# Attention and a squared-ReLU feed-forward layer on one core: the scores of a tile written as two operations, and a new order of all work

## The chip, the cores and the metric

The kernel runs on one core of a Trainium2 chip. The metric is the time of one execution on the device in microseconds (us). Each version is run several times, and the median of its runs is its time.

## The reference

Two things are computed, one after the other. First, attention with 4 batches, 8 heads, 768 tokens and 64 numbers per head. A token sees the first 8 tokens of its batch ("global" keys) and itself with the 95 tokens before it ("local" keys):

```python
scores = (1.0 / np.sqrt(D)) * np.matmul(q, k.transpose(0, 1, 3, 2))
rel = pos[:, None] - pos[None, :]
is_global = pos[None, :] < 8
is_local = (rel >= 0) & (rel < 96)
keep = is_global | is_local
dist = np.where(is_global & ~is_local, 96.0, np.abs(rel))
scores = scores - slopes[:, None, None] * dist        # slopes[h] = 2 ** -(h + 1)
a = softmax(np.where(keep, scores, -1e9))
attn = np.matmul(a, v)                                # (4, 8, 768, 64)
```

Then the result, with the heads side by side, is a matrix x of 3072 tokens by 512, and goes through a feed-forward layer:

```python
h = x @ w_in                  # (3072, 512) @ (512, 2048)
g = np.maximum(h, 0.0) ** 2
out = g @ w_out               # (3072, 2048) @ (2048, 512), fp32
```

## The kernel before, in words

**Tiles and blocks.** The 3072 tokens are cut into 24 tiles j of 128, six to a batch. Since a token sees at most 95 tokens back, a tile's scores need only the keys of tile j itself and of the tile to its left, j - 1, into which the 8 global keys of the batch are copied. The first tile of each batch (0, 6, 12, 18) has no left one. Two tiles make a block of the feed-forward layer, so there are 12 blocks.

**The order of the work.** The program first only collects operations. Each has a name, the engines that may execute it, and a function that emits its instructions. `Plan.run` (L33) then emits them in the order of a string, `ORDER` (L57 to L161). A word of it is name.arguments, and may be followed by #n (the n-th operation of that name), by : and digits (which of the eight PSUM banks it takes, a digit each), and by @ and a letter for the engine (A is ACT, V is DVE, P is POOL; without one, the first engine that the operation lists). Every engine executes its words in the order in which they are written; between engines, a word waits for the words whose tiles it reads or overwrites. A PSUM bank is one tile, so a word that opens a bank waits until the last reader of what was in it is done.

**The words of attention.** ld (L307) and load (L310) are loads that POOL issues: ld.q.j, ld.k.j, ld.v.j and the pieces of the weights, ld.win and ld.wout, first; load.j later for a whole tile. tr.0.j and tr.1.j transpose q and k of a tile on PE (L506, four matmuls) and T.0.j and T.1.j copy the result out of PSUM (L429 on ACT, L433 on DVE); from tile 8 on, T.j is one transposing DMA issued by SP (L537). warm (L532) is eight matmuls on zeros. bias.j.g (L579, tiles 0 to 2 alone) writes slopes and mask into PSUM, and the scores are added on top. sc.j.g (L599) computes scores, matmuls of 64 rows each: 16 for a tile with a left neighbour, 8 without. They go to four banks (two without a neighbour): for each group g of four heads one bank for the even heads and one for the odd ones. `SETS` says which groups g make one operation; where it has no entry, all groups of a tile are one (L612). exp.j.odd.g (L665, ACT) is the exponential of one bank, mul.j.g (L690, DVE) multiplies a group's two exponentials with a table of decay and mask, E or E0 (built by the words E0.n). pv.j.h (L748) multiplies half of the heads with the values, and norm.j.h (L778 and L779, DVE) divides by the sum. gk, kl and gv are small copies of global keys, of a left tile's keys and of global values; gate.j is a small operation behind which POOL's loads are held back. trx.j (L816) and xT.j transpose x on PE for the first eight tiles; later xT.j is a transposing DMA of SP (L840).

**The words of the feed-forward layer.** Blocks 0 and 1 compute the first product directly: s1.blk.s (L1061, sixteen matmuls, in whole or in parts #1 to #4), then relu and sq. From block 2 on the first product is done in seven products instead of eight (sums of quarter matrices are multiplied, and the results added): xs (L922) and isum (L888) make the sums of x and of w_in, h.blk.half.p1 to p7 (L950, eight matmuls each) are the products, u copies a product out (L429), c adds another and applies the ReLU (L995 on DVE, L865 on ACT), and q squares (L1015, ACT, or L1017, DVE). The second product is direct in block 0 (s2.0, L1339); from block 1 on it too is seven products, s2.blk.p1 to p7, each in pieces .0 and .1 of four matmuls (L1212), with wsum (L1132) and sum (L1167) for the sums. part and o copy or add its results (L429, L1287), and st stores a row tile of out through SP (L1309). In the last block the stores are in pieces, and the last o of a row tile is cut at column 192 (`LASTCUT`), so that it has 64 columns and its store 32 KB.

Lines that the prediction speaks of are thus those of PE (L506 transposition, L532 warm, L599 scores, L748 values, L950 first product, L1061 direct first product, L1212 and L1339 second product), of DVE (L433, L690, L778, L779, L995, L1287) and of the DMAs (L307, L840, L1309).

Of the kernel before, what the change touches and what calls it, by code (L numbers as in the profile page):

```python
# [63 lines left out]
tr.0.4:7 ld.q.5 ld.v.4 norm.2.1 mul.3.1 relu.0.6@A s1.0.3#2 gv.2@P pv.3.0:3 norm.3.0 trx.2:5 T.0.4@A pv.3.1:6  # L64
ld.win.1.0 norm.3.1 ld.win.0.1 xT.2@A sc.4.0:1047 exp.4.1.1 exp.4.1.0 tr.1.5:3 T.1.5@A s1.0.2:5 trx.3:6 xT.3@V
ld.win.0.0 ld.win.5.0 s1.0.2#2 s1.0.2#3 s1.0.2#4 relu.0.3@V exp.4.0.1 ld.v.5 gv.3@P exp.4.0.0 gk.4@V sq.0.6@V
relu.0.2@A s1.1.3:7 ld.win.7.0 relu.1.3@A load.6 s1.1.6:0 mul.4.1 tr.0.5:6 mul.4.0 sq.0.3@V s1.1.2:3 T.0.5@A ld.wout.3
pv.4.0:2 ld.wout.1 sq.0.2@V sc.5.0:4157 ld.wout.0 s1.0.4:6 relu.1.2@A exp.5.1.1 s1.0.1:3 sq.1.3@A exp.5.0.0 relu.0.4@V
s1.1.4:7 ld.wout.2 norm.4.0 pv.4.1:4 gv.4@P norm.4.1 sq.0.4@A load.7 exp.5.1.0 sq.1.2@A relu.1.4@A s1.0.0:6 gate.9
ld.wout.4 mul.5.0 s1.0.0#2 sq.1.4@A s1.0.0#3 s1.1.5:2 trx.4:1 exp.5.0.1 relu.1.6@V s1.1.1:4 ld.wout.5 s1.0.1#2  # L70
relu.1.1@A E0.1 mul.5.1 relu.1.5@A pv.5.0:7 s1.1.7:0 s1.1.0:5 sq.1.1@V norm.5.0 ld.wout.6 E0.0 sq.1.5@V tr.1.6:4
sq.1.6@A pv.5.1:2 relu.1.7@A tr.0.6:7 s1.0.0#4 norm.5.1 xT.4@A sq.1.7@A h.2.0.p2:0 ld.wout.7 T.1.6@V h.2.1.p2:1
trx.5:2 xT.5@V relu.1.0@A sq.1.0@A gate.14 h.2.0.p1:5 xs.2.0 s1.0.5:4 sum.1.2 s1.0.7:2 relu.0.1@A xs.2.1 gate.10
sum.1.0 sum.1.1 relu.0.0@A T.0.6@A sc.6.0:36 wsum.0.0 sum.1.3 sq.0.0@A sq.0.1@A s2.0.0.0:7 relu.0.7@A s2.0.1.0 load.9
exp.6.0.0 xs.2.2 s2.0.2.0 exp.6.1.0 s2.0.3.0 s2.0.0.1:2 s2.0.1.1 wsum.2.0 relu.0.5@A sq.0.7@A s2.0.2.1 load.8 mul.6.0
wsum.1.0 s2.0.3.1 tr.0.7:3 tr.1.7:6 gate.15 isum.0.0 h.2.1.p1:4 T.0.7@A s2.0.4.0 isum.0.1 s2.1.p1.0:3 isum.3.1 T.1.7@A
sq.0.5@A pv.6.0:6 isum.1.1 s2.0.4.1 s2.0.5.1 u.2.0.1@A c.2.0.c11 s2.0.5.0 gate.11 u.2.1.1@A h.2.1.p6 q.2.0.c11@A
isum.1.0 T.8 s2.0.6.1 u.2.1.2@A s2.0.6.0 isum.3.0 pv.6.1:0 h.2.0.p6 wsum.2.1 wsum.0.1 s2.1.p1.1 s2.0.7.1 c.2.1.c11
norm.6.0 gate.13 o.0.1@V st.0.1 s2.0.7.0 h.2.1.p7 part.1.p1@A s2.1.p6.0 u.2.0.2@A o.0.0@A u.2.1.3@A h.2.0.p7 h.2.1.p4
T.9 norm.6.1 wsum.3.0 u.2.0.3@A sc.7.0:1762 c.2.1.c21@A wsum.1.1 h.2.1.p5:0 c.2.1.c22 q.2.1.c11@A s2.1.p2.0:4  # L80
exp.7.1.0 exp.7.0.0 isum.2.1 load.10 h.2.0.p4 exp.7.0.1 mul.7.0 exp.7.1.1 s2.1.p2.1 isum.2.0 s2.2.p1.0:7 q.2.1.c21@A
mul.7.1 h.2.0.p5:1 s2.1.p6.1 part.1.p6@A trx.6:6 gate.12 c.2.0.c21@A load.12 pv.7.0:2 xT.6@A c.2.0.c22 q.2.1.c22@A
q.2.0.c22@A s2.2.p1.1 h.2.1.p3 s2.1.p7.0 wsum.3.1 o.1.p2 norm.7.0 h.2.0.p3 pv.7.1:5 s2.1.p7.1 q.2.0.c21@A st.0.0
c.2.1.c12 s2.1.p5.0 s2.1.p5.1 part.1.p7@A q.2.1.c12@A s2.1.p4.0 T.10 s2.1.p4.1 c.2.0.c12 gk.7@V q.2.0.c12@A o.1.p5
o.1.p4@A sc.8.0:6201 st.1.1 part.2.p1@A s2.1.p3.0 norm.7.1 sum.2.0 sum.2.1 s2.1.p3.1 trx.7:5 xT.7@V o.1.p3 h.3.0.p1:3
exp.8.1.0 gk.8@V h.3.1.p1:2 exp.8.0.0 exp.8.1.1 exp.8.0.1 h.3.0.p2:6 xs.3.0 u.3.1.1@A sc.9.0:1540 s2.2.p6.0 mul.8.0
xs.3.1 mul.8.1 u.3.0.1@A h.3.0.p6 exp.9.0.1 exp.9.1.1 gv.7@V h.3.1.p2:4 c.3.0.c11 h.3.1.p6 c.3.1.c11 exp.9.0.0
# [1344 lines left out]
```

## Time and profile before

| | |
|---|---|
| runs of before | 199.14, 200.15, 200.28 us; median 200.15 us |
| span of the profiled execution | 197.6 us (2.55 us under the median of the runs) |
| PE, TensorE's matmuls | busy 191.9 us, 97% of the span |
| PEld, TensorE's weight loads (beside matmuls) | 169.6 us, 86% |
| DVE | 173.2 us, 88% |
| ACT | 163.0 us, 82% |
| POOL | 80.4 us, 41% |
| DMA traffic | 26.91 MB, mean 136 GB/s |

The span is that of one execution taken by the hardware profiler. The runs are timed around the whole launch, and so are a little longer than the span. A row of the profile gives, after line, engine and operation, what is written and read (bank is PSUM; bank numbers are left out), the shape, and how often; in the groups by line follow busy time and the mean in ns of one, then the idle time of the engine just before such instructions and what ended it. In the chain of waits and in the order of time, the first number is the start in us, the second the duration (in the chain, the time until the next step). PE is busy whenever a matmul is under way, also where that matmul waits for its weights.

### The profile page before, as it was taken

The page shows a single profiled execution, that of the slowest core. Times are in us where ns is not written, and L with a number is a line of the kernel's source. Part 1 is how long each engine was busy: PE and PEld are TensorE (multiplying, and loading weights), DVE is VectorE, ACT ScalarE, POOL GpSimd, SP SyncE. Part 2 cuts the span into 40 slices and gives each one's busy share as a digit, 9 for nine tenths or more (in the row PEclk, how much of TensorE's full clock was granted, in tenths as well). Part 3 has the DMA queues.
Part 4 walks back from the last instruction along what each step waited for, and adds up shares of the span by engine and source line. Part 5 has one row for each costly group of instructions (what it writes and reads, how often), then busy time and mean ns, then how long its engine had stood idle before and what let it go on. Part 6 is the DMA issues. An engine that isn't in the chain of part 4 may idle for free.

```text
span 197.6 us, 6777 instructions
## 1 busy us (share of the span) xinstructions
PE 191.9 (97%) x2776; PEld 169.6 (86%) x2776; DVE 173.2 (88%) x423; ACT 163.0 (82%) x335; POOL 80.4 (41%) x101
## 2 busy tenths in 40 slices
...
GB/s 127 153 158 171 181 181 185 182 202 159 139 209 191 75 200 88 145 174 210 151 129 203 114 124 194 160 121 92 136 81 116 154 55 56 27 30 163 0 106 106
DMA packets 111857, 26.91 MB, mean 136 GB/s; under 512 B 103379, under 2 KB 109011, under 8 KB 111827
## 3 DMA queue, kind: packets, MB, share of 16 engines
...
## 4 chain that ended last, share of the span: by engine, by line
PE 95%; DVE 2%; issue 1%; ACT 0%; DVEq 0%
PE bank L1212 35%; PE bank L950 32%; PE bank L1061 7%; PE bank L599 6%; PE bank L748 5%; PE bank L1339 4%; PE bank L372 2%; PE bank L506 2%; PE bank L532 1%; DVE qkT L433 1%; PE bank L816 1%; PE bank L579 0%; ACT qkT L429 0%; DVE o L1287 0%; DVE v L433 0%
## 5 line engine op out<-in xcount | busy, mean ns | idle before, releaser
L1015 ACT ACTIVATE hs<-hr 128x512 bf16<-128x512 f32 x72 | 44.8, 641 | 5.1 <-DVE hr L995 4.7
L665 ACT ACTIVATE esc<-bank 128x512 bf16<-128x512 f32 x78 | 42.9, 614 | 1.3 <-PE bank L599 1.0
L1212 PE MATMUL bank<-wsum,hsum 128*128 128x256 bf16 x264 | 36.2, 273 | 0.0
L1212 PEld LDWEIGHTS <-hsum 128*128 128x128 bf16 x360 | 32.1, 98 | 4.1 <-issue 0.5
L995 DVE CUSTOM_DVE_ANT_0 hr<-bank,early 128x512 f32<-128x512 f32 x45 | 30.4, 685 | 2.5 <-PE bank L950 1.5
L950 PEld LDWEIGHTS <-win 128*128 128x128 bf16 x480 | 29.7, 98 | 1.0
L950 PEld LDWEIGHTS <-qk_first 128*128 128x128 bf16 x480 | 29.7, 98 | 1.0
L429 ACT COPY early<-bank 128x512 f32<-128x512 f32 x42 | 24.5, 591 | 3.6 <-PE bank L950 3.3
L690 DVE TENSOR_TENSOR at<-esc,E 128x1024 bf16<-128x1024 bf16 x39 | 26.7, 696 | 0.1
L1212 PEld LDWEIGHTS <-hs 128*128 128x128 bf16 x264 | 24.0, 98 | 2.6
L310 POOL DMA_DIRECT2D qk<-in_q_dram x18 | 16.0, 890 | 21.9 <-DMA qkT<-qk 20.6
L1212 PE MATMUL bank<-wout,hs 128*128 128x256 bf16 x176 | 24.9, 273 | 0.0
L310 POOL DMA_DIRECT2D v<-in_v_dram x18 | 16.0, 888 | 18.3 <-DVE v L480 14.9
L950 PE MATMUL bank<-xT,win 128*128 128x128 bf16 x320 | 23.4, 219 | 0.0
L431 POOL COPY v<-v 8x520 bf16<-8x520 bf16 x8 | 5.7, 718 | 43.3 <-PE bank L748 43.3
L950 PE MATMUL bank<-xs,qk_first 128*128 128x128 bf16 x320 | 22.8, 219 | 0.0
L779 DVE TENSOR_TENSOR x<-bank,rs 128x256 bf16<-128x256 f32 x48 | 20.4, 425 | 1.7
L865 ACT ACTIVATE hr<-bank 128x512 f32<-128x512 f32 x33 | 19.4, 598 | 1.3 <-PE bank L950 0.4
L748 PE MATMUL bank<-v,at 128*128 128x65 bf16 x352 | 17.8, 193 | 0.0
L1287 DVE TENSOR_TENSOR o<-bank,part 128x256 f32<-128x256 f32 (+2 forms) x34 | 13.8, 410 | 3.3 <-PE bank L1212 3.2
L429 ACT COPY part<-bank 128x256 f32<-128x256 f32 x29 | 10.9, 375 | 7.1 <-PE bank L1212 6.9
L310 POOL DMA_DIRECT2D qk<-in_k_dram x18 | 16.1, 897 | 0.9 <-DMA win<-in_moe_w_in_dram 0.5
...
## 6 DMA issues: line engine op xcount, KB each, us to landing
out_dram<-o SPq DMA_DIRECT2D x22, 256.0 KB, 2.5
v<-in_v_dram POOLq DMA_DIRECT2D x24, 128.0 KB, 5.6
qk<-in_q_dram POOLq DMA_DIRECT2D x18, 128.0 KB, 5.0
qk<-in_k_dram POOLq DMA_DIRECT2D x18, 128.0 KB, 5.8
wout<-in_moe_w_out_dram POOLq DMA_DIRECT2D x8, 256.0 KB, 8.5
win<-in_moe_w_in_dram POOLq DMA_DIRECT2D x6, 256.0 KB, 6.9
qk_first<-in_k_dram POOLq DMA_DIRECT2D x5, 128.0 KB, 5.6
qk_first<-in_q_dram POOLq DMA_DIRECT2D x5, 128.0 KB, 5.7
```

Source lines behind the costliest of these rows:

```text
L310: nc.gpsimd.dma_start(out=dst, in_=src)
L429: nc.scalar.copy(dst, src)
L665: nc.scalar.activation(out=tiles[tag, j, g][:, odd], in_=tiles.pop(("sc", j, odd, g)).rearrange("p a c -> p (a c)"), func=Act.Exp, scale=s ...
L690: nc.vector.tensor_mul(at, tiles.pop(("esc", j, g)), bias)
L748: nc.tensor.matmul(out=po[:, hi, :], lhsT=tiles["at", j, g][:, odd, at * P : (at + 1) * P], rhs=v_sb[kj][:, h, :], start=(i == 0), stop=(i ...
L779: nc.vector.tensor_tensor(out=x[:, 4 * hf : 4 * hf + 4, :], in0=po[:, :, :D], in1=rs.to_broadcast([P, 4, D]), op=Alu.mult,)
L865: nc.scalar.activation(dst, src, Act.Relu)
L950: nc.tensor.matmul(out=tiles["h", blk, g, bank][:, n], lhsT=left_[:, s, k], rhs=right_[:, k], start=opens and n == 0 and k == 0, stop=k == ...
L995: nc.vector._custom_dve(TENSOR_ADD_SAT, out=hr, in0=src, in1=tiles.pop(("u", blk, g, i)), s0=float("inf"), s1=0.0,)
L1015: nc.scalar.activation(hs, hr, Act.Square)
L1061: nc.tensor.matmul(out=hT[:, c, cols], lhsT=w_in_sb[s][:, kt, c * P : (c + 1) * P], rhs=tiles["xT", blk][:, kt, cols], start=(kt == 0), st ...
L1212: nc.tensor.matmul(out=tiles["acc", blk, bank][:, cols], lhsT=left_[:, s], rhs=right_[:, cols], start=first and s == 0, stop=s == NSTEP - ...
```

## The change

Three things are changed.

`SETS` gets an entry for every tile that has a left neighbour: its two groups of four heads are now an operation each. Such a tile has two words sc.j.0 and sc.j.1 of eight matmuls and two banks in place of one of sixteen matmuls and four banks, and tiles 1 and 2 have two bias words each. That makes 44 score words where there were 24, and 5 bias words where there were 3. The number of matmuls is the same. The exponentials, products and values of a tile are as before, but each now depends on the word of its own group.

The order is written anew from end to end: the words' sequence on all engines, the banks that they take, and the order of the loads. Some small words change engines: counted by kind, DVE takes over five u, three q, four T, a gv and a c, and gives up three gk, two o, two part, a relu, an xT and a kl. The written order of before ends with pieces of block 11 and its 64-column last o; that of after ends with s2.10.p4.1, o.10.p4 and st.10.1, a store of a whole row tile (256 KB).

The warm word records which bank it takes, as others do; `Plan.run` does not read that.

The diff, with the part of the order that is spoken of:

```diff
--- before.py
+++ after.py
 ORDER = """
-tr.0.0:0 warm:7 tr.1.0:1 T.1.0@V bias.0.0:23 T.0.0@A sc.0.0 ld.win.3.0 exp.0.0.0 ld.k.1 tr.1.1:4 bias.1.0:5670 T.1.1@V ld.q.1
-tr.0.1:1 ld.v.0 exp.0.1.0 T.0.1@V sc.1.0 exp.1.0.1 pv.0.0:2 ld.q.2 tr.0.2:3 norm.0.0 ld.k.2 T.0.2@V ld.k.3 exp.1.1.1
-pv.0.1:4 tr.1.2:1 bias.2.0:7203 ld.v.1 norm.0.1 exp.1.1.0 ld.q.3 tr.1.3:6 gk.1@A T.1.2@A sc.2.0 exp.1.0.0 T.1.3@V
-ld.k.4 pv.1.0:4 ld.v.2 gk.2@V exp.2.1.0 exp.2.1.1 norm.1.0 trx.0:1 xT.0@A ones.6 pv.1.1:5 tr.0.3:6 T.0.3@V exp.2.0.0
-tr.1.4:2 ld.win.6.0 sc.3.0:4361 ld.q.4 norm.1.1 ld.v.3 trx.1:7 gv.1@V exp.2.0.1 exp.3.0.0 pv.2.0:5 exp.3.1.0 exp.3.0.1
-T.1.4@V xT.1@V pv.2.1:0 ld.k.5 ld.win.2.0 exp.3.1.1 gk.3@A ld.win.2.1 norm.2.0 s1.0.3:2 mul.3.0 s1.0.6:4 ld.win.4.0
...
-xT.11 s2.4.p2.0:2 h.5.0.p1:3 q.4.0.c22@A o.3.p5 mul.12.0 c.4.0.c12 o.3.p4@A c.4.1.c21@A u.5.0.1@A c.4.1.c12 T.15
...
-exp.13.0.0 T.14 s2.4.p2.1 c.5.0.c11 exp.13.1.0 pv.12.1:1 q.5.0.c11@A s2.4.p1.0:5 xs.5.0 sum.4.0 pv.12.0:7 xs.5.1
...
-part.11.p6@A s2.11.p2.0:6 st.10.1 s2.11.p2.1 sum.11.2#2 o.11.p2 s2.11.p7.0 s2.11.p7.1 part.11.p7@A sum.11.3 s2.11.p5.0
-s2.11.p5.1 o.11.p5 st.11.1 st.11.0 sum.11.3#2 s2.11.p4.0 s2.11.p4.1 o.11.p4@A st.11.1#2 s2.11.p3.0 s2.11.p3.1
-s2.11.p3.0#2 o.11.p3 s2.11.p3.1#2 st.11.0#2 o.11.p3#2 st.11.0#3
+ones.6 tr.0.0:0 warm:1 ld.k.1 ld.q.1 tr.0.1:1 tr.1.0:2 bias.0.0:34 tr.1.1:5 T.1.0 E0.0 T.1.1 T.0.0@A T.0.1 bias.1.1:67
+sc.0.0 bias.1.0:02 ld.k.2 ld.q.3 ld.q.2 tr.0.2:5 sc.1.0 sc.1.1 exp.0.1.0 exp.0.0.0 exp.1.0.0 ld.v.0 pv.0.0:1 norm.0.0
+exp.1.0.1 exp.1.1.1 T.0.2 gk.1 ld.k.3 tr.1.3:4 T.1.3 exp.1.1.0 pv.0.1:3 tr.1.2:0 T.1.2 bias.2.0:61 norm.0.1 bias.2.1:57
+sc.2.1 sc.2.0 exp.2.1.1 exp.2.0.0 trx.0:4 gk.2@A ld.q.4 xT.0 tr.0.3:2 T.0.3 ld.k.4 ld.v.1 pv.1.0:0 ld.v.2 ld.k.5
+pv.1.1:3 tr.1.4:7 ld.win.0.1 norm.1.0 norm.1.1 gv.1 exp.2.1.0 exp.2.0.1 tr.0.4:4 T.0.4 sc.3.1:62 sc.3.0:10 ld.win.0.0
+ld.q.5 ld.win.6.0 exp.3.1.1 ld.v.3 ld.win.3.0 T.1.4 ld.win.4.0 ld.v.4 ld.win.1.0 load.6 pv.2.0:5 norm.2.0 ld.win.2.0
+gk.3@A exp.3.0.1 ld.win.2.1 trx.1:3 sc.4.0:24 sc.4.1:67 pv.2.1:5 mul.3.1 ld.v.5 exp.3.0.0 exp.3.1.0 ld.win.5.0 norm.2.1
+mul.3.0 gate.9 gv.2 s1.0.0:1 tr.1.5:0 s1.0.0#2 xT.1@A s1.0.0#3 s1.0.0#4 gk.4@A trx.2:3 exp.4.0.1 exp.4.1.1 mul.4.1 T.1.5
+load.7 exp.4.0.0 ld.win.7.0 ld.wout.1 ld.wout.0 load.8 T.8 ld.wout.2 tr.0.5:5 T.0.5 s1.0.6:6 pv.3.0:7 pv.3.1:2 norm.3.0
+gv.3 norm.3.1 relu.0.0 xT.2@A exp.4.1.0 sq.0.0 sc.5.0:10 sc.5.1:53 s1.0.3:4 s1.0.3#2 gate.12 trx.3:7 mul.4.0 exp.5.1.1
+exp.5.0.1 s1.0.4:2 exp.5.0.0 relu.0.3@V xT.3 ld.wout.4 exp.5.1.0 sq.0.3 relu.0.6 relu.0.4 ld.wout.3 mul.5.1 pv.4.0:3
+norm.4.0 gate.11 sq.0.4 pv.4.1:5 sq.0.6@V norm.4.1 E0.1 s1.1.3:4 relu.1.3 sq.1.3@V s1.1.4:1 relu.1.4 gv.4@A s1.0.1:7
+s1.0.1#2 trx.4:0 relu.0.1 s1.1.1:3 sq.0.1@V sq.1.4@V relu.1.1 sq.1.1 s1.1.0:6 s1.0.2:2 ld.wout.5 s1.0.2#2 s1.0.2#3
...
+T.12 xT.9 s2.1.p3.1 c.3.1.c12 c.3.0.c21 mul.10.1 o.1.p3 sc.11.1:02 sc.11.0:31 sc.12.0:45 mul.10.0 s2.2.p6.0 exp.11.0.0
...
+norm.11.1 h.4.1.p4 c.4.1.c21 st.1.1 xT.11 sum.3.3 o.2.p3 kl.14@A h.4.1.p3 h.4.0.p5:2 c.4.0.c22 q.4.0.c22 c.4.1.c12
...
+st.2.0 s2.3.p6.1 s2.3.p2.0:6 xs.5.0 xs.5.1 mul.12.0 sum.3.2 part.3.p6 gk.13 exp.13.0.0 pv.12.0:5 h.4.0.p3 norm.12.0
...
+c.4.0.c21 mul.13.0 q.4.0.c21@V h.5.1.p6 u.5.1.2 s2.3.p4.0 sc.14.0:24 pv.13.1:0 exp.14.0.0 exp.14.1.0 gate.20 s2.3.p5.1
...
+norm.13.0 sum.4.0 u.5.0.3 h.5.1.p4 c.5.1.c21 q.5.1.c21 q.5.1.c11 norm.13.1 mul.14.0 load.17 h.5.1.p5:4 s2.3.p3.1 o.3.p3
+h.5.0.p5:5 c.5.1.c22 sc.15.1:20 sc.14.1:76 exp.15.1.1 exp.14.0.1 exp.15.0.1 st.3.0 xT.13 st.2.1 c.5.0.c22 T.19 s2.3.p4.1
...
+norm.14.0 c.5.1.c12 s2.4.p2.0:2 s2.4.p2.1 s2.4.p1.1 c.5.0.c21 sc.16.1:35 sc.15.0:67 sc.16.0:14 part.4.p1 s2.4.p6.0
...
+sum.5.2 sum.5.3 sc.17.0:16 sc.17.1:07 sc.19.0:42 h.6.1.p3 c.6.1.c12 q.6.0.c12 exp.17.0.0 exp.17.1.0 exp.17.0.1
...
+c.7.1.c21 sc.18.0:26 sc.19.1:31 sc.20.0:70 q.7.1.c22@V h.7.0.p7 exp.18.0.0 s2.6.p1.0:5 s2.6.p2.0:2 s2.6.p1.1 exp.19.1.1
...
+s2.7.p1.1 part.7.p1 sc.20.1:37 sc.21.0:04 sc.21.1:12 exp.20.0.1 xs.9.0 xs.9.1 h.9.1.p1:5 s2.7.p2.0:3 s2.7.p6.0 s2.7.p6.1
...
+o.9.p4 s2.10.p7.0 c.11.1.c21 st.9.0 sum.11.0 sum.11.2 sum.11.1 st.9.1 q.11.1.c12 sum.11.0#2 sum.11.1#2 sum.11.3
+s2.10.p7.1 s2.10.p5.1 part.11.p1 s2.11.p6.0 s2.11.p6.1 part.10.p7 o.10.p5 s2.10.p3.0 s2.10.p3.1 s2.11.p2.0:4 sum.11.2#2
+q.11.1.c21@V part.11.p6 s2.11.p2.1 s2.11.p7.0 s2.11.p7.1 sum.11.3#2 o.10.p3 st.10.0 o.11.p2 s2.11.p5.0 s2.11.p5.1
+part.11.p7 s2.11.p4.0 s2.11.p4.1 o.11.p4 o.11.p5 s2.11.p3.0 st.11.0 st.11.1 st.11.1#2 s2.11.p3.1 o.11.p3 st.11.0#2
+s2.11.p3.0#2 s2.10.p4.0 s2.11.p3.1#2 o.11.p3#2 st.11.0#3 s2.10.p4.1 o.10.p4 st.10.1
 """
...
-    SETS = {}
+    SETS = {j: [(0,), (1,)] for j in range(NT) if j % TPB}
...
             def emit_warm(e):
...
-            plan.op(("warm",), {"PE": 0.216 * NKEEP}, emit_warm, key=base)
+            wusers = []
+            wusers.append(plan.op(
+                ("warm",), {"PE": 0.216 * NKEEP}, emit_warm, key=base, takes=(*G, [wusers]),
+            ))
```

174 lines of the change are left out of this document (79 added, 95 removed).

## The prediction

> **What bounds the kernel now.** I read the totals first, then busy time by stretch, then the chain that ended last, and the order of time at both ends.
>
> ```profile
> span 197.6 us, 6777 instructions
> PE 191.9 (97%) x2776; PEld 169.6 (86%) x2776; DVE 173.2 (88%) x423; ACT 163.0 (82%) x335; POOL 80.4 (41%) x101
> ...
> 0.00:20.00 20.00, 17.46 (x206) 12.39 (x207) 12.02 (x51) 13.26 (x30) 19.20 (x28) 1.00 1.81 153
> 20.00:194.00 174.00, 174.00 (x2570) 157.06 (x2567) 160.56 (x372) 149.71 (x306) 61.23 (x74) 1.00 1.20 134
> 190.00:198.00 8.00, 4.39 (x47) 3.84 (x45) 2.64 (x8) 1.00 (x3) 0.00 (x0) 1.00 0.37 131
> ```
>
> The third to sixth columns of the stretches are PE, weight loads, DVE and ACT. From 20 to 194 us PE never rests, at a granted clock of 1.00. So the kernel is as long as PE's list of work, plus PE's waits in the first 20 us, plus what follows PE's last product. DVE, at 160.6 of 174, is close behind and has little room.
>
> A busy PE is not a PE at its peak, so I take paces from the chain of waits: start to start, where nothing is waited for.
>
> ```profile
> 4.79 0.85 PE bank L506 x4
> 5.64 2.41 PE bank L532 x8
> ...
> 34.39 0.22 PE bank L506 x4
> 34.62 0.24 PE bank L748 x8
> ...
> 36.46 0.45 PE bank L950 x8
> ...
> 38.66 0.33 PE bank L599 x8
> 38.99 3.56 PE bank L1339 x16
> ...
> 43.44 0.43 PE bank L1339 x2
> ...
> 47.61 0.44 PE bank L1212 x4
> ...
> 50.69 0.55 PE bank L599 x16
> 51.24 0.55 PE bank L950 x8
> ```
>
> Columns: start, pace, line, matmuls. A product of phase one (L950) takes 0.45, a piece of phase two (L1212) 0.44, half a tile's values (L748) 0.24, a bf16 transposition 0.22. Paced in this way, a word of the order has a **place**: 4.58 us (PE's first transposition, below) plus the paces ahead of it. The place of the first s1 word is 16.0; the trace has it at 18.12.
>
> ```profile
> 4.58 1.06 PE L506 MATMUL bank<-ident,plain 128*128 128x128 f32 x4
> ...
> 11.62 0.23 PE L599 MATMUL bank<-qkT 64*128 64x128 bf16 x2 [0.52 <-DVE qkT L433]
> ...
> 18.12 1.49 PE L1061 MATMUL bank<-xT,win 128*128 128x128 bf16 x16
> ```
>
> So the start loses 2.1 us, in waits such as that of 0.52 for a copy of q and k. Everything between 21 and 193 us loses next to nothing. That bounds any gain: PE's work does not shrink by one matmul.
>
> **Scores side by side.** After 16 score matmuls (0.55) the next product takes 0.55 instead of 0.45: together 0.65 of PE. After 8 (0.33) the sixteen of L1339 take 3.56, where 8 x 0.43 are 3.46: together 0.43. Eight more matmuls thus cost 0.22, and every run of score matmuls, which use 64 rows, costs 0.43 - 0.22 = 0.21 beside them, for going in and out. The order of before has 24 such runs. In the new one the 44 score words stand in 21: 11 with 12, 14.1 with 15.1, 15.0 with 16, 17 with 19.0, 18 with 19.1 and 20.0, 20.1 with 21. The halves of a tile stand in one run but for tiles 14, 15, 19 and 20, whose halves have other tiles' beside them, so that only 14.0 is a new run of its own. 3 x 0.21 = **0.6 us less**. The score matmuls and the bias matmuls stay as many.
>
> **The start.** The loads on POOL's queue are in another order: q, k and v of the first tiles ahead, every piece of w_in later.
>
> ```profile
> 5.69 1.80 POOL L307 DMA_DIRECT2D qk_first<-in_k_dram  x2
> ...
> 17.32 1.06 POOL L307 DMA_DIRECT2D v<-in_v_dram  x1
> ...
> qk_first<-in_k_dram POOLq DMA_DIRECT2D x2, 128.0 KB, 5.6
> ...
> v<-in_v_dram POOLq DMA_DIRECT2D x1, 128.0 KB, 6.7
> ```
>
> The second of the two at 5.69 starts half of 1.80 later, at 6.6, is seventh of the queue, and lands 5.6 us after, at 12.2. The seventh is k of tile 3 in the new order too, but there PE transposes it at place 11.4, ahead of pv.0.1 and tr.1.2, which wait behind it: 0.8 lost. The load of v.4 at 17.32 is twentieth and lands at 24.0. In the new order v.4 is twentieth behind the same bytes (fifteen loads of q, k and v, three whole pieces of w_in, two halves), and pv.4.0 needs it at place 22.5: at least 1.5 lost by then, and w_in's piece 4 just ahead of it asks for as much. DVE adds its own wait.
>
> ```profile
> L995 DVE CUSTOM_DVE_ANT_0 hr<-bank,early 128x512 f32<-128x512 f32 x45 | 30.4, 685 | 2.5 <-PE bank L950 1.5 <-ACT esc L665 0.2 <-ACT early L429 0.2
> L690 DVE TENSOR_TENSOR at<-esc,E 128x1024 bf16<-128x1024 bf16 x39 | 26.7, 696 | 0.1
> L779 DVE TENSOR_TENSOR x<-bank,rs 128x256 bf16<-128x256 f32 x48 | 20.4, 425 | 1.7
> L1287 DVE TENSOR_TENSOR o<-bank,part 128x256 f32<-128x256 f32 (+2 forms) x34 | 13.8, 410 | 3.3 <-PE bank L1212 3.2
> L778 DVE RECIPROCAL rs<-bank 128x4 f32<-128x4 f32 x48 | 8.4, 175 | 2.2 <-PE bank L748 2.1
> L433 DVE COPY qkT<-bank 128x512 bf16<-128x512 bf16 x7 | 2.9, 418 | 1.9 <-PE bank L506 1.9
> ```
>
> ```profile
> 185.50 1.29 DVE L995 CUSTOM_DVE_ANT_0 hr<-bank,early 128x512 f32<-128x512 f32 x2 [0.40 <-PE bank L950]
> ```
>
> Two L995 take 1.29, so the next starts 0.60 after one that lasts 0.685: on DVE I count 0.08 less than a row's mean. The new order has E0.0 ahead of T.1.1, and four T more on DVE than before. From trx.0 (place 13.5) to T.0.5 DVE has four norm (0.55, reciprocal and product), three mul (0.60), and five T, an xT, two gv and a gate (2.7 together, at L433's price): 6.7 us. With 0.5 for the ends of trx.0 and T.0.5 that is place 20.7, and sc.5.0, which needs T.0.5, stands at 19.9: another 0.8 behind the first 0.8, and beside the 1.5 of the loads, not on top. For the small waits that both orders have for copies I add 0.4 and take 2.0 lost, against 2.1 before: **-0.1**, with bounds of -0.6 (only the 1.5 of v.4 holds) and +0.4 (loads and DVE add up in part).
>
> **The middle.** Counted by kind, DVE takes over five u, three q, four T, a gv and a c, and gives up three gk, two o, two part, a relu, an xT and a kl: 4 us more work in all, nearly all of it in the first 40 us. From place 45 to 175 both orders give DVE the same within 1 us, but unevenly. The tightest spot is xs.5.0, for which tile 11's x must be back from SP's transposition.
>
> ```profile
> L840 SPq DMA_TRANSPOSE xT<-x x16: 1189/1196/2084, 66.9 to 172.8; - x16
> ...
> DMA to landing us min/median/max: 2.4/3.2/5.1
> ```
>
> norm.11.1 stands at place 78.0; its 0.5 us and the median landing of 3.2 make x ready at 81.7. From xs.5.0 to o.3.p3 the new order has on DVE four mul, three c, two sum and two q (0.60 each, as L690 and L995), four norm (0.55), three o (0.33), and three xs, a kl, a gk and two gates (an estimated 1.3 together, from L690's 1024 columns in 0.6): 11.1 us, to 92.9. The scores sc.14.1, whose bank o.3.p3 empties, stand at 92.9. So nothing is lost at 3.2, 1.2 at the 4.3 that the trace has for this very transposition (below), 1.9 at 5.1. Before, norm.11.1 and xs.5.0 stood 6.9 us apart, now 5.0. Elsewhere exp.19.0.1, which empties the bank of pv.18.0, comes 0.2 late behind the exps of three tiles that now stand together, and some ten more words of PE stand within 0.1 of what they wait for. I take **+0.6**, between 0 (all transpositions at 3.2, ACT's 0.2 made good) and +2.4 (5.1 at tile 11 and 0.5 more behind it), nearer the lower end, since fewer loads surround this one than before.
>
> **The end.** Before, the last piece is 64 columns, and its store 32 KB. The new order puts s2.10.p4.1, a whole piece, last; o.10.p4 is a copy on ACT, and st.10.1 stores both halves of the row tile, 256 KB.
>
> ```profile
> 193.38 0.37 ACT L429 COPY o<-bank 128x256 f32<-128x256 f32 x1 [1.38 <-PE bank L1212]
> ...
> 194.57 0.28 PE L1212 MATMUL bank<-wout,hsum 128*128 128x64 bf16 x4 [0.45 <-DVE o L1287]
> 194.88 0.22 DVE L1287 TENSOR_TENSOR o<-bank,part 128x64 f32<-128x64 f32 x1 [0.37 <-PE bank L1212]
> ...
> out_dram<-o SPq DMA_DIRECT2D x1, 32.0 KB, 1.4
> ...
> out_dram<-o SPq DMA_DIRECT2D x2, 256.0 KB, 2.2
> ```
>
> From PE's last end (194.57 + 0.28) it is 0.25 to the end of the addition, 1.4 to the landing, and 1.1 to the end of the span: 2.75. Now the copy takes 0.37 for 0.22 and the store 2.2 (two whole ones at 190.3) for 1.4: 0.15 + 0.8, rounded down **+0.9**, between +0.6 and +1.3. The wait of 0.45 stays: s2.11.p3.0#2 writes the bank that o.11.p3 reads, and stands right behind it; the four matmuls of s2.10.p4.0 could cover it, but stand behind that word on PE. The Trainium skill (DMA: Bandwidth & Descriptors, Anatomy of one DMA) gives a DMA about 2.0 us whatever its size, plus its bytes at 436 GB/s. By that the two stores would differ by an estimated 0.5 us and not 0.8, and the sum would be 0.3 lower; its fixed part is not in this trace, where the small store has landed after 1.4.
>
> **The sum.** -0.6 - 0.1 + 0.6 + 0.9 = +0.8 us on a span of 197.6. The runs have a median of 200.15, 2.55 above this span; I keep that difference: **201.0**. End by end that is -0.6 - 0.6 + 0 + 0.6 to -0.6 + 0.4 + 2.4 + 1.3, so 199.5 to 203.7; either extreme needs all parts to fall together.
>
> **The rivals.** First, the late transpositions decide (slower). Where loads of POOL are under way, this trace has a transposition of q and k at 7.4:
>
> ```profile
> qk<-in_k_dram POOLq DMA_DIRECT2D x1, 128.0 KB, 7.4
> qkT<-qk SPq DMA_TRANSPOSE x1, 7.4
> ```
>
> ```profile
> xT<-x SPq DMA_TRANSPOSE x1, 4.3
> ```
>
> The first two rows are of the stretch from 90.3 to 90.5, the third, tile 11's, of 85.6 to 85.8. From the last norm of tiles 15, 19 and 21 to their xs it is now 4.9, 2.9 and 5.5 us of place, where it was 7.3, 5.2 and 7.7. At 5.1 tile 11 costs 1.9, and the other three an estimated 0.4 each, since each delay gives the next one time: +3.1 in place of +0.6, **203.5**. It decides from 4.5 us at tile 11 on. Against it: load.13 and load.14 stand at places 71 and 61, before at 77 and 84, and may be through by then; that makes it a fifth and not a half. The Trainium skill (DMA: Bandwidth & Descriptors, Issuing engines are not separate DMA queues) says that DMAs from all engines run on the same 16 DMA engines and interleave. By that rule, which the two rows of 7.4 bear out, any load at that moment would slow this transposition.
>
> Second, the start closes up (faster). If the first landings come earlier with a 128 KB load at the queue's head, and DVE's chain hides in what is left, 1.5 of the 2.1 go, and the middle keeps its slack: -0.6 - 1.5 + 0 + 0.9 = -1.2, **198.95**. For it: the attention of five tiles is ahead of every s1 word. Against it: fifteen loads and five pieces of weights must pass one queue either way.
>
> Third, the change doesn't do what it says: each score word pays for going in and out, adjacent or not. Then 44 instead of 24 pay 0.21, +4.2 in place of -0.6, **205.8**. Against it: inside one word of before the two groups already follow each other without a gap (eight more for 0.22).
>
> **Chances.** Forecast 0.60, late transpositions 0.20, closed start 0.15, words that pay 0.05. A measurement of this kernel tells about 1%, 2 us, from no change. Under 198.15: a third of the closed start, and 0.03 of the forecast: 0.08. Over 202.15: three quarters of the late transpositions, the words that pay, and 0.04 of the forecast: 0.24. Within: 0.68. The range reaches down to the closed start's own lower part, 198.9, and up to the late transpositions, 203.5.
>
> **What would show it.** Right: score runs of 24 matmuls at 0.77, with one entry and exit each; PE without rest from about 25 us on, with the first s1 word near 18.5; a last ACT copy, then a store of 256 KB that lands after about 2.2; PE's end near 194.8. Wrong: a wait of PE of over 0.5 us between places 80 and 160, led by xs or T; an s1 word under 18 us, or no wait for the seventh load; a store at the end that lands as fast as the small one.

## The result and the profile after

After takes 211.95 us (median of four runs, 209.75 to 213.03), before 199.95 us in the same comparison: the ratio is 1.059, interval 1.052 to 1.066. Medians are of all executions; ratios and intervals, here and below, leave out those over 1.5% longer than the fastest of their kernel. The profiled execution of after has a span of 209.9 us, 12.3 more than before. The prediction said 201.0 us, within 198.9 to 203.5.

The top of the page of after, busy time first, then PE and its granted clock in 40 slices of 5.2 us:

```profile
span 209.9 us, 6776 instructions
PE 195.4 (93%) x2773; PEld 169.8 (81%) x2776; DVE 176.4 (84%) x426; ACT 160.9 (77%) x335; POOL 78.3 (37%) x98
...
PE   7998999994999999779999988999999989999992
...
PEclk9999999998899999999999999999999999999998
```

PE's matmuls are as many as before (2776 weight loads in both; of after's matmuls three have left no record), but PE no longer works without rest between 20 and 194 us. It has a hole near 50 us, with a lower clock just behind it, and shallower ones near 85, 92, 126 and 170. DVE, ACT and POOL are busy for a smaller share of the span than before (84, 77 and 37%): nothing has become the new bound by its own work. The same by stretches (PE is the second number, DVE the fourth, the clock the seventh):

```profile
0.00:20.00 20.00, 17.96 (x228) 12.48 (x228) 14.05 (x57) 13.73 (x32) 19.20 (x28) 1.00 1.84 149
20.00:40.00 20.00, 19.87 (x295) 17.57 (x295) 17.81 (x46) 19.40 (x39) 16.18 (x21) 1.00 1.91 178
40.00:60.00 20.00, 16.86 (x193) 11.95 (x194) 15.30 (x33) 14.59 (x30) 9.12 (x11) 0.91 1.98 163
60.00:80.00 20.00, 19.74 (x297) 17.74 (x295) 18.45 (x40) 18.23 (x40) 9.64 (x11) 1.00 2.18 166
80.00:100.00 20.00, 17.56 (x265) 15.39 (x263) 16.68 (x46) 14.28 (x29) 7.67 (x9) 1.00 1.16 143
...
120.00:140.00 20.00, 18.38 (x286) 16.56 (x285) 18.48 (x42) 15.26 (x33) 5.89 (x7) 1.00 1.02 128
```

Set against the places of the prediction (PE's words paced end to end), the trace of after is late by 2.2 us at 24 us, where before was by 2.3. Then it loses 4.8 between 45 and 54 us, 3.7 between 79 and 98, 0.2 near 112, 1.9 between 125 and 128, 0.8 in small waits from 138 to 163, and 1.1 at 170. The 0.6 in the end is in both. These terms are 12.4 more than before. PE's last end, at 206.46 us and not 194.85, is 11.6 later, which is 12.2 with the 0.6 less for the score runs; the 0.2 between the two are the error of the paces. With 0.7 more behind PE's last product the 11.6 make the 12.3 of the span.

**The hole at 50 us.** The chain of waits of after, from 36 to 58 us:

```profile
33.13 8.41 DMA qk<-in_k_dram
...
41.62 8.93 DMA qkT<-qk
50.55 0.05 issue
50.60 0.81 PE bank L598 x16
51.40 2.67 PE bank L1338 x6
```

and the first of these scores in the order of time:

```profile
50.60 0.23 PE L598 MATMUL bank<-qkT 64*128 64x128 bf16 x2 [2.98 <-DMA qkT<-qk]
```

PE's scores of tile 8 (L598) wait for T.8, SP's transposition of q and k of that tile. T.8 is issued at 41.62, when load.8 has landed, and lands 8.93 later. Before, T.8 was issued at 51.5 and the scores ran at 59.0. The new order has brought sc.8.0 forward from place 57.1 to 45.6, T.8 has come forward by only 9.9 us, and it takes more than twice as long. With the time of before it would have landed at 45.3, ahead of its reader: PE stands idle only from 47.6 on. So the wait comes from the 5.2 us by which T.8 is longer. These are the rows of T.8 itself, first of before, then of after:

```profile
qkT<-qk SPq DMA_TRANSPOSE x1, 3.7
```

```profile
qkT<-qk SPq DMA_TRANSPOSE x1, 8.9
```

The second part of the loss is in the clock, the seventh column again:

```profile
47.00:49.00 2.00, 0.62 (x12) 0.44 (x8) 2.00 (x5) 0.87 (x2) 1.77 (x3) 1.00 2.49 144
49.00:50.50 1.50, 0.00 (x0) 0.00 (x0) 0.24 (x1) 0.00 (x0) 0.85 (x1) 1.00 2.96 115
50.50:52.00 1.50, 1.40 (x18) 0.83 (x19) 0.00 (x0) 0.97 (x3) 1.03 (x2) 0.63 1.39 205
52.00:54.00 2.00, 2.00 (x7) 0.74 (x6) 1.85 (x3) 1.08 (x3) 2.00 (x3) 0.50 1.98 167
54.00:56.00 2.00, 1.95 (x29) 1.76 (x29) 1.23 (x3) 1.27 (x3) 0.48 (x1) 0.92 2.36 150
```

PE stands for 3.0 us, and 0.3 us after it has resumed, its clock falls to half until about 54 us: three words of L1338 take 2.67, where three at 0.43 are 1.3. In the clock's record the half clock lasts 3.41 us, from 50.89 to 54.30, so it costs 1.7 us beyond the wait.

**The holes near 85 and 92 us.** SP's queue, then DVE's, in order of time:

```profile
77.83 1.23 SPq L536 DMA_TRANSPOSE qkT<-qk  x1
79.16 0.53 SPq L1308 DMA_DIRECT2D out_dram<-o  x1
```

```profile
82.76 0.43 DVE L1286 TENSOR_TENSOR o<-bank,part 128x256 f32<-128x256 f32 x1 [1.29 <-DMA out_dram<-o]
...
89.64 0.42 DVE L429 COPY part<-bank 128x256 f32<-128x256 f32 x1
91.79 0.42 DVE L921 TENSOR_TENSOR xs<-xT 128x512 bf16<-128x512 bf16 x1 [1.73 <-DMA xT<-x]
92.25 0.29 DVE L921 TENSOR_TENSOR xs<-xT,xs 128x256 bf16<-128x256 bf16 x1
92.46 0.69 DVE L689 TENSOR_TENSOR at<-esc,E 128x1024 bf16<-128x1024 bf16 x1
```

The store st.1.0 stands behind T.13 on SP, and T.13 waits there for its load until 77.8. So the store goes out at 79.16, its o buffer comes free 3.5 us later, and o.2.p5 holds DVE for 1.29. Three words behind it is mul.11.1, for which PE's pv.11.1 then waits 1.1. Ten microseconds on, xs.5.0 holds DVE for 1.73, until tile 11's x is back, and mul.12.0, which has long had its exponentials, stands behind it. PE waits for that too:

```profile
93.20 0.29 PE L747 MATMUL bank<-v,at 128*128 128x65 bf16 x4 [1.18 <-DVE at L689]
```

At 123 us xs.7.0 does the same to c.6.1.c12, and at 168 us xs.10.0 to u.10.1.1. In the waits of DVE, after has two entries that before did not have at all:

```profile
DVE xs L921 <- DMA xT<-x: 6.3, 6, 1.7
...
DVE o L1286 <- DMA out_dram<-o: 2.7, 2, 1.4
```

### The profile page after: what moved, and what is told of

Its sections match the earlier page's. It is cut to its first block, busy times and chain, and to the rows that moved or that the text cites. A ratio compares the mean times of both kernels' runs of the same rounds, so it can differ in the third digit from the quotient of the medians.

```text
span 209.9 us, 6776 instructions
## 1 busy us (share of the span) xinstructions
PE 195.4 (93%) x2773; PEld 169.8 (81%) x2776; DVE 176.4 (84%) x426; ACT 160.9 (77%) x335; POOL 78.3 (37%) x98
## 4 chain that ended last, share of the span: by engine, by line
PE 40%; DMA 25%; DVE 15%; POOL 11%; issue 4%; ACT 2%; SPq 0%; DVEq 0%; POOLq 0%
PE bank L1211 19%; PE bank L949 15%; DMA xT<-x 12%; DMA qkT<-qk 4%; POOL qk_first L303 4%; DMA qk<-in_k_dram 4%; DMA win<-in_moe_w_in_dram 4%; DVE hsum L1166 3%; DVE hr L994 2%; PE bank L1338 2%; DVE at L689 2%; POOL win L303 2%; POOL v L303 2%; PE bank L747 2%; DVE xs L921 2%
## 5 line engine op out<-in xcount | busy, mean ns | idle before, releaser
L1014 ACT ACTIVATE hs<-hr 128x512 bf16<-128x512 f32 x69 | 43.1, 638 | 10.6 <-DVE hr L994 10.4
L664 ACT ACTIVATE esc<-bank 128x512 bf16<-128x512 f32 x78 | 43.6, 606 | 7.7 <-PE bank L598 4.2
L1211 PEld LDWEIGHTS <-hsum 128*128 128x128 bf16 x360 | 32.6, 98 | 4.1 <-issue 0.6
L1211 PE MATMUL bank<-wsum,hsum 128*128 128x256 bf16 x264 | 35.3, 273 | 0.0
L949 PEld LDWEIGHTS <-win 128*128 128x128 bf16 x480 | 30.3, 98 | 3.7 <-issue 1.9
L425 ACT COPY early<-bank 128x512 f32<-128x512 f32 x41 | 23.6, 591 | 3.5 <-PE bank L949 3.2
L949 PE MATMUL bank<-xs,qk_first 128*128 128x128 bf16 x320 | 24.1, 219 | 1.7 <-DVE early L429 0.9
L1211 PE MATMUL bank<-wout,hs 128*128 128x256 bf16 x176 | 23.5, 272 | 0.0
L747 PEld LDWEIGHTS <-at 128*128 128x128 bf16 x352 | 14.6, 98 | 5.0 <-DVE at L689 2.8
L427 POOL COPY v<-v 8x520 bf16<-8x520 bf16 x5 | 3.2, 637 | 40.8 <-PE bank L747 40.8
```

Of the source, the lines that this page charges most:

```text
L425: nc.scalar.copy(dst, src)
L664: nc.scalar.activation(out=tiles[tag, j, g][:, odd], in_=tiles.pop(("sc", j, odd, g)).rearrange("p a c -> p (a c)"), func=Act.Exp, scale=s ...
L747: nc.tensor.matmul(out=po[:, hi, :], lhsT=tiles["at", j, g][:, odd, at * P : (at + 1) * P], rhs=v_sb[kj][:, h, :], start=(i == 0), stop=(i ...
L949: nc.tensor.matmul(out=tiles["h", blk, g, bank][:, n], lhsT=left_[:, s, k], rhs=right_[:, k], start=opens and n == 0 and k == 0, stop=k == ...
L1014: nc.scalar.activation(hs, hr, Act.Square)
L1211: nc.tensor.matmul(out=tiles["acc", blk, bank][:, cols], lhsT=left_[:, s], rhs=right_[:, cols], start=first and s == 0, stop=s == NSTEP - ...
```

## The experiments

My theory was late data: the halves of the scores cost nothing, and the new order puts the readers of transpositions, loads and stores too near behind them. The main rival was that the 44 score words cost PE time of their own. Line numbers differ by a few between kernels.

**The split alone.** The order of before, with both halves where the one word stood:

```diff
-    SETS = {}
+    SETS = {j: [(0,), (1,)] for j in range(NT) if j % TPB}
-... sc.6.0:36 ... sc.7.0:1762 ...
+... sc.6.0:36 ... sc.7.0:17 sc.7.1:62 ...
```

> The order of before, with only the scores (and the biases of tiles 1 and 2) written as two operations of two banks, both standing where the one stood. Late data (my theory: what the new order does to transpositions and loads costs the 12 us, the halves nothing): as before, 200.0 within 0.6 us. Rival, words that pay (each of the 44 score words costs 0.2 of PE or a wait of its own): about 204.

Measured: 199.07 against 199.72 us, ratio 0.9972, interval 0.9942 to 1.0002. The halves cost nothing.

**The order alone.** After, with the halves joined where they stand side by side:

```diff
-    SETS = {j: [(0,), (1,)] for j in range(NT) if j % TPB}
+    SETS = {j: [(0,), (1,)] for j in (1, 2, 14, 15, 16, 19, 20)}
-... sc.8.0:75 sc.8.1:13 ...
+... sc.8.0:7513 ...
```

> The new order, with the halves joined to one operation of four banks wherever both stand side by side (13 of the 20 tiles that have two groups; the halves of tiles 1, 2, 14, 15, 16, 19 and 20 stay). Late data: as after, 211.9 within 1 us. Rival, words that pay: 13 of 20 extra words gone, about 2.6 us less, 209.3.

Measured: 212.84 us, ratio 1.062, interval 1.053 to 1.071. It is as slow as after, with the halves of seven tiles still apart. With the run before, this puts the 12 us on the order, which here means everything that was rewritten with it: the sequence, the banks, the loads and the engines of small words.

**Work for PE while it waits.** After, with 12 matmuls ahead of tile 8's scores:

```diff
+            if (j, gs[0]) == (8, 0):
+                for _ in range(12):
+                    nc.tensor.matmul(out=psum(), lhsT=ident, rhs=w_out_sb[0][:, 0], start=True, stop=True)
             for g, pair, at, kt, odd in todo(gs):
```

> After, with 12 more matmuls (512 columns each, about 2.6 us) on PE ahead of the scores of tile 8, into a bank that the scores overwrite; they need nothing that is late. Idle clock (theory: the 3 us in which PE waits for tile 8's transposition are followed by about 3.5 us at a granted clock of 0.5, which cost 1.9 more): the granted clock stays at 1.00 through 49 to 58 us, the six L1338 that took 0.43 each at full clock take it again, and the whole is 1.5 to 2 us shorter, near 210.2, though PE has 2.6 us more to do. Rival (those matmuls are slow for their own sake, from weights that have just landed): same as after, 211.9, or up to 0.5 longer.

Measured: 211.93 us (ratio 1.058, interval 1.052 to 1.065), as after, and not the 1.5 to 2 us less that the theory asked for. The same stretches as above, of this kernel:

```profile
49.00:50.50 1.50, 1.50 (x15) 0.62 (x14) 0.30 (x1) 0.00 (x0) 1.45 (x3) 1.00 1.53 189
50.50:52.00 1.50, 1.50 (x21) 0.81 (x15) 0.17 (x1) 1.29 (x3) 1.50 (x3) 1.00 1.49 193
52.00:54.00 2.00, 1.95 (x29) 1.65 (x29) 1.97 (x4) 1.98 (x5) 1.49 (x2) 1.00 2.29 158
```

PE has full clock, but that does not show that the extra matmuls kept it up. The traces of the order alone, and of two kernels below (words moved ahead, the end as before), have the same words of PE in front of these scores, but for joined halves, and no extra matmuls: T.8 lands after 7.6 or 7.7 us, PE waits 0.8 to 1.1 us, and the clock stays at 1.00. The slow clock is thus not part of every execution of this order, and where T.8 lands early, the extra matmuls only delay the scores (here T.8 has landed at 49.6, after a wait that would have been 2.0, and the scores start at 50.28). Whether the clock would have fallen here without them is not shown.

What the half clock is worth in the median can be read from the mean granted clock of after's four executions: it was 1.00 in the shortest, 209.75 us, and 0.987 to 0.990 in the others, 211.88 to 213.03. In the profiled one, with 0.987, the 3.41 us at half clock take 0.008 off the mean. So three of the four probably had it, and the median of after contains it.

**Fewer loads.** After, without the loads of q and k of tiles 9 and 10:

```diff
                 load_v(j)
+                if j in (9, 10):
+                    return
                 load_part(0, j)
```

> After, with the loads of q and k of tiles 9 and 10 left out (four of 128 KB; these two tiles compute on what earlier tiles left in the buffers). Late data by traffic (theory: the transposition of tile 8 takes 8.9 us because loads are in flight): it takes 5 to 6.5 us, PE's wait at tile 8's scores falls from 3.0 to under 1 us, the clock stays up, tile 9 and 10's transpositions come earlier too, and the whole is 4 to 5 us shorter, near 207.5. Rival (this transposition is slow whatever else is in flight, or load 8 itself is what is late): it stays at 8 to 9 us and the whole within 1 us of after.

Measured: 214.54 us, ratio 1.068 (1.061 to 1.075): slower, and T.8 took longer:

```profile
qkT<-qk SPq DMA_TRANSPOSE x1, 10.4
```

```profile
49.00:52.00 3.00, 0.00 (x0) 0.00 (x0) 1.04 (x2) 0.00 (x0) 0.41 (x1) 0.79 1.41 98
52.00:54.00 2.00, 1.83 (x19) 1.09 (x20) 0.07 (x1) 1.19 (x3) 0.87 (x2) 0.50 1.40 76
54.00:56.00 2.00, 2.00 (x9) 0.88 (x8) 1.97 (x4) 0.86 (x2) 1.76 (x3) 0.50 1.78 49
```

The expectation failed on a mistake in the experiment: without loads to wait for, T.9 and T.10 were issued at 43.1 and 47.3 instead of 51.4 and 58.2, and shared the time with T.8. They took 13.8 and 13.4, and the loads issued from 39.6 to 41.2 took 12 to 14, where before has 8 to 8.7. Taking loads away is no test while it lets other transpositions in. It does show what the next two runs needed: a transposition is heavy traffic itself.

**Loads held back.** After, with one word moved so that POOL waits until T.8 is done:

```diff
-... ld.wout.5 ... load.10 ... load.11 h.3.1.p2:1 ...
+... load.11 ld.wout.5 ... load.10 ... h.3.1.p2:1 ...
```

> After with one word moved: load.11 to ahead of wout.5 on POOL's queue. It overwrites what T.8 reads, so POOL stands there until T.8 is done, and only wout.2, 4 and 3 are in flight beside T.8. Theory (loads in flight make T.8 slow): T.8 takes 4 to 6 us where after's executions show 7.6 to 8.9, and PE's wait at tile 8's scores is under 0.5. The loads behind come 6 us later, PE waits for them instead (wout.5 and tile 9), so the whole is longer than after, 214 to 218. Rival (T.8 is slow by itself): 7.6 or more.

Measured in a single execution: 221.54 us. Beside T.8 were wout.2, 4 and 3, and also the v of tile 11, the first of load.11's three loads, which does not wait for T.8 (issued at 38.05, landed 8.2 us later). T.8 took

```profile
qkT<-qk SPq DMA_TRANSPOSE x1, 5.8
```

The time of T.8 came as the theory has it, and PE no longer waits for tile 8's scores. The whole is longer than I said, 214 to 218, since PE now waits elsewhere:

```profile
PE bank L1334 <- DMA wout<-in_moe_w_out_dram: 6.5, 2, 5.8
PE bank L594 <- DMA qkT<-qk: 2.8, 2, 2.3
PE bank L743 <- DVE at L685: 2.0, 1, 2.0
```

Around each of the longest waits, of 5.8, 2.3 and 2.0 us, the clock fell to 0.50, for 6.83, 3.41 and 3.41 us. What is in flight beside a transposition sets how long it takes: the same T.8 took 3.7 us in before, 5.8 here, and 7.6 to 8.9 in the order of after.

**The same collision in the order of before.** One word moved, load.8 to behind wout.4:

```diff
-... ld.wout.4 ... load.9 ... load.8 mul.6.0 ...
+... ld.wout.4 load.8 ... load.9 ... mul.6.0 ...
```

> The order of before with one word moved: load.8 from behind load.9 to behind wout.4, so that T.8 (which SP issues as soon as that load has landed) falls among the loads of wout.5 to 7 and of tile 9, as in after; the scores of tile 8 stay where they are, 10 us later. Theory (a transposing DMA among loads takes 7 to 9 us and holds the loads up as well, and what made after slow is that its reader stands too near): T.8 takes 7 us or more in place of 3.7, load.9 lands later than 8.0 us after its issue, and the whole is as before within 0.7 us. Rival (such a transposition costs the whole kernel time wherever its reader stands, because the loads behind it come late): over 2 us longer than before.

Measured: 201.23 against 199.54 us, ratio 1.0082 (1.0047 to 1.0116). T.8 is nearly as slow as in after:

```profile
qkT<-qk SPq DMA_TRANSPOSE x1, 8.2
```

```profile
PE bank L1333 <- DMA wout<-in_moe_w_out_dram: 2.5, 2, 2.2
```

The scores of tile 8 stand 10 us later than in after and do not wait for it. The loads of q and k of tile 9 landed 9.8 and 9.7 us after their issue, where before has 8.0, and PE does not wait for them either. The 1.7 us that were lost anyway have another cause in the trace: load.8 has three loads, which now stand ahead of wout.5 on POOL, and PE waits for wout.5, which landed 7.9 us after its issue, so it was not slower than such loads in before (8.5 in the median), but issued later. I had left that out, so "within 0.7" failed, and so did "over 2".

**Transpositions of tiles 8 and 9 on PE.**

```diff
-    JQK, JX = 8, 8
+    JQK, JX = 10, 8
-... T.8 ... T.9 ... isum.2.1 s2.0.3.0 ... gk.8@A load.11 ...
+... isum.2.1 tr.0.8:7 tr.1.8:1 T.0.8@A T.1.8 s2.0.3.0 ... gk.8@A tr.0.9:6 tr.1.9:3 T.0.9@A T.1.9 load.11 ...
```

> After, with q and k of tiles 8 and 9 transposed on PE and copied by ACT and DVE, in place of SP's transposing DMA (PE gets 16 matmuls more, 0.9 us). Late data: PE's wait of 3.0 at tile 8 and the slow clock behind it go, 4.9 less and 0.9 more of work; the next thing to be late is tile 10's load, 1 to 1.5. The whole near 209. Rival (the loads of tile 8 themselves are late, not the transposition): PE waits as long at the transposition on PE, the whole within 1 us of after or longer.

Measured: 209.62 us, ratio 1.050 (1.043 to 1.056). The ratios of the two kernels to before differ by 1.9 us, near what was expected, but their intervals overlap (after has 1.052 to 1.066), and after's one execution at full clock, 209.75, was as short as these. So the gain is not clear of the noise, and how much of it is the half clock that no longer comes is not shown. The loads behind got faster. Loads issued from 38.9 to 43 us, first of after, then of this kernel from 39.7 to 43.5:

```profile
v<-in_v_dram POOLq DMA_DIRECT2D x1, 128.0 KB, 11.7
qk<-in_q_dram POOLq DMA_DIRECT2D x1, 128.0 KB, 11.1
```

```profile
v<-in_v_dram POOLq DMA_DIRECT2D x1, 128.0 KB, 8.0
qk<-in_q_dram POOLq DMA_DIRECT2D x1, 128.0 KB, 8.0
```

**Words moved ahead of those that wait.** After, on SP and DVE alone:

```diff
-... T.13 st.1.0 ... xs.5.0 xs.5.1 mul.12.0 sum.3.2 part.3.p6 gk.13 ...
+... st.1.0 T.13 ... mul.12.0 sum.3.2 part.3.p6 gk.13 xs.5.0 xs.5.1 ...
-... xs.7.0 sum.5.2 sum.5.3 ... c.6.1.c12 ... xs.9.0 xs.9.1 ... mul.20.1 ... xs.10.0 mul.22.1 ... xs.10.1 u.10.1.1@V ...
+... sum.5.2 sum.5.3 ... c.6.1.c12 xs.7.0 ... mul.20.1 xs.9.0 xs.9.1 ... mul.22.1 ... u.10.1.1@V xs.10.0 xs.10.1 ...
```

> After, with words moved on queues alone: the store st.1.0 ahead of T.13 on SP; on DVE mul.12.0, sum.3.2 and gk.13 ahead of xs.5.0 and xs.5.1; sum.5.2, sum.5.3 and c.6.1.c12 ahead of xs.7.0; mul.20.1 ahead of xs.9.0 and xs.9.1; mul.22.1 and u.10.1.1 ahead of xs.10.0 and xs.10.1. No work is added or removed. Late data (theory: in-order queues stand behind late transpositions, and PE then waits for what is queued behind them): of the 7 us that PE loses between 75 and 175 us, 3 to 5 go, the whole near 208. Rival (DVE has no room, its work is late anyway): within 1 us of after.

Measured: 208.2 us, ratio 1.042 (1.035 to 1.049): by the ratios 3.4 us less than after, clear of the noise, with not one instruction added or removed. Nor is it the clock: in executions with a mean clock of 0.997 or more, after, the order alone and the end as before took 209.75 to 214.65 us, this kernel 207.49 to 208.76. DVE had the room; its queue had the wrong word at its head. The waits at pv.11.1 and pv.12.0 are gone; a wait of 1.5 for DVE's norm has come up at 91.6 us, behind xs.5.0, which now holds DVE for 2.65. Which of the five moves gave how much was not tried.

**The end as before.**

```diff
-... s2.11.p3.0#2 s2.10.p4.0 s2.11.p3.1#2 o.11.p3#2 st.11.0#3 s2.10.p4.1 o.10.p4 st.10.1
+... s2.10.p4.0 s2.10.p4.1 o.10.p4 st.10.1 s2.11.p3.0#2 s2.11.p3.1#2 o.11.p3#2 st.11.0#3
```

> After, with the end in the manner of before: s2.10.p4.0 and .1, o.10.p4 and its store stand ahead of s2.11.p3.0#2, so that the last store is the 32 KB one; the two pieces cover PE's wait for o.11.p3. Theory: 0.9 of the last store and 0.4 of the wait go, about 1.2 us less than after. Rival (the end is set by the store's issue, whatever its size): under 0.4.

Measured: 212.46 us, ratio 1.066 (1.059 to 1.073): no gain is seen. PE's wait for o.11.p3 is gone in the trace, but the large store is still issued near the end, at 206.8, and the small one right behind it at 207.2, so that from PE's last end to the end of the span it is 3.4 us, where after has 3.5. In this trace the 0.9 of the last store has not gone. In the times, with intervals of 0.7% (1.4 us) to either side, neither the 1.2 us that I expected nor the rival's 0.4 could be told from nothing.

**The three together** (tiles 8 and 9 on PE, words moved ahead, the end as before):

> The last three together: words moved on DVE and SP, the end of before, tiles 8 and 9 transposed on PE. If the causes add: 211.9 - 4 - 1.2 - 3 = 203.7; still not faster than before, since the other transpositions of x stay late and the start loses as much as it did. If DVE and not the transpositions is short of time: over 207.

Measured: 205.84 us, ratio 1.031 (1.025 to 1.037). By the ratios that is 5.6 us less than after, clear of the noise; the single gains, 3.4 and 1.9, add to 5.3. It is 2.1 more than the 203.7 that I had expected, for which each of the three gains had been put too high. PE's granted clock is 1.00 in every stretch of 20 us of it. About 6.5 us to before remain; the profiled execution is 7.4 longer than that of before. Of these 7.4, 0.9 are the added matmuls of the transpositions, 4.4 are further waits (tr.1.8 for norm.7.1, 0.9; h.9.1.p6 for xs.9.1, which this kernel itself has moved back, 0.8; smaller ones), and the end is 2.7 longer, with one store of 32 KB that took 3.7 us in this execution; the 0.6 of the score runs go the other way. Further moves were not tried, so which part of the new order the remaining time belongs to is read from the trace alone.

**A shorter end for the order of before.** The split kernel of the first run, with two pieces moved between the last words:

```diff
-... s2.11.p4.0 s2.11.p4.1 o.11.p4@A st.11.1#2 s2.11.p3.0 s2.11.p3.1 s2.11.p3.0#2 ...
+... s2.11.p3.0 s2.11.p3.1 s2.11.p4.0 s2.11.p4.1 o.11.p4@A st.11.1#2 s2.11.p3.0#2 ...
```

> The order of before with the scores as two operations side by side (the kernel of the first run) and one thing at the end: s2.11.p4.0 and .1 with o.11.p4 and its store stand between s2.11.p3.1 and s2.11.p3.0#2, so that PE has 0.87 us of work while o.11.p3 empties its bank, a wait of 0.45 before. Theory: 0.5 us less than that kernel, a ratio to before near 0.995. Rival (the last store is issued behind one more store on SP and gives it back): 0.997 to 1.0.

Measured: 200.34 against 199.54 us, ratio 1.0029 (1.0006 to 1.0053): the gain did not come, and the kernel lies above the split alone (0.9942 to 1.0002).

```profile
192.94 0.84 PE L1207 MATMUL bank<-wout,hsum 128*128 128x192 bf16 x8 [0.57 <-DVE o L1282]
...
195.21 0.28 PE L1207 MATMUL bank<-wout,hsum 128*128 128x64 bf16 x4 [0.45 <-DVE o L1282]
```

The pieces had been the cover of another wait: s2.11.p3.0 now waits 0.57 for o.11.p5. The 0.45 stays, for s2.11.p3.1#2, which still stands right behind the word that lets o.11.p3 go. The lowest ratio of the study is that of the split alone, and it cannot be told from before.

## Why the prediction was wrong, step by step

**Score runs: right.** The prediction asked for runs of 24 matmuls at 0.77. The chain of waits of after has

```profile
73.08 0.78 PE bank L598 x24
```

The 0.6 us themselves were not timed alone: the split in the order of before merges no runs of different tiles.

**The start: right in sum.** 2.2 us lost at 24 us against 2.0 said, the first s1 word at 18.38 against "near 18.5". Inside it one landing was off. The loads of the first tiles landed after 4.8 us in place of the 5.6 that I took over from before, where a 256 KB piece stood at the queue's head. So the seventh load came in time, and the losses lie elsewhere in the same 15 us: that the sum fits is in part luck.

**The middle: wrong, and this is the step that failed.** It said 0.6, between 0 and 2.4; it was about 12.4. Three things in it failed. The runs show 3.4 us for the third and about 1.9, not clear of the noise, for the first; for the rest there are the traces alone.

First, the list of what is late was incomplete. The prediction followed the loads of the first tiles and the transpositions of x, and of some ten more words it said only that they stand within 0.1 of what they wait for. T.8 was not on the list. Its reader had moved from place 57.1 to 45.6, 11.5 us earlier, T.8 itself only 9.9, and among the loads it took 8.9 in place of 3.7. That is 3.0 of wait and 1.7 of half clock in the profiled execution; transposing it and tile 9 on PE gave about 1.9 us by the ratios.

Second, a landing time was carried over from one moment to another. I priced the transposition of x at 3.2 to 5.1, from the landings of the same kind in before. For tile 11 that held, with 4.3. But the x issued at 103.9 us took 7.4, that at 117.6 took 5.4, and the same T.8 took 3.7, 5.8 and 8.9, by what else is in flight. The rule of the Trainium skill (DMA: Bandwidth & Descriptors, Issuing engines are not separate DMA queues), that all DMAs share the same 16 engines and interleave, agrees with this: SP's transposition and POOL's loads delay each other, the loads from 8.0 to 11.7 us. I had used it for the rival alone, and not for the forecast.

Third, waits were priced one by one against PE. A wait on an in-order queue is paid by everything behind it: the store behind T.13, mul.12.0 behind xs.5.0, c.6.1.c12 behind xs.7.0. At xs.5.0 I had even forecast the wait (1.2 to 1.9; it was 1.73), but looked for its effect at sc.14.1, 11 us of DVE later, and not at the next word. Moving the words gave 3.4 us back.

**The clock: not foreseen.** In the trace of before PE waits at most 1.2 us, so nothing in it showed what follows a long wait. The Trainium skill (TensorE: Matmul & The Clock Gate, Part 1) says that PE's clock falls to half after an idle window of about 3.4 us, which runs freely, and comes back after as long a busy one. The traces agree with the length: within each trace the changes of the clock lie whole multiples of 3.41 us apart, and the half clock inside a kernel lasted 3.41 us or twice that. They do not agree with an idle window, and here the measurement decides. The fall came around waits of 5.8, 3.7, 3.0, 2.3 and 2.0 us, and not around others of 2.0 (the end as before) and 2.2 (load.8 moved). It came at the end of a stretch of 3.41 us in which PE was busy little: for 0.43 us of it in after, 1.06 in fewer loads, 0, 1.19 and 1.43 in loads held back. In the two traces without a fall PE was still busy for 1.67 and 1.54 of such a stretch. So it matters not only how long a wait is, but also where in the stretch it lies.

**The end: right.** From PE's last end to the end of the span it is now 3.49 us, 0.7 more than before; said were 0.9, between 0.6 and 1.3. The last two stores landed 1.4 us (32 KB) and 2.0 us (256 KB) after their issue. The figures that the prediction set beside its 0.8, a fixed 2.0 us and the bytes at 436 GB/s (the Trainium skill, DMA: Bandwidth & Descriptors, Anatomy of one DMA), are fitted there to DMAs that GpSimd issues, and these stores are SP's: the difference of 0.6 is near the 0.5 estimated by them, the fixed part is not seen. The wait of 0.45 stayed, as forecast:

```profile
205.19 0.28 PE L1211 MATMUL bank<-wout,hsum 128*128 128x64 bf16 x4 [0.45 <-DVE o L1286]
...
206.49 0.37 ACT L425 COPY o<-bank 128x256 f32<-128x256 f32 x1 [2.00 <-PE bank L1211]
```

**The rivals.** "Late transpositions decide" named the mechanism and the side, with a chance of 0.20 and 203.5 us. Its price was too small, 3.3 us over before where 12.0 were measured, since it had four transpositions of x and neither T.8 nor the words queued behind. The start did not close up: the first s1 word came at 18.38, not under 18. "Words that pay" is refuted by the first two runs.
